# A run of products in 64x128, 32x128, 128x64, 128x32 and full tiles inside a fused attention and feed-forward kernel

## The chip, the cores and the metric

The kernel runs on one core of a Trainium2 chip. A core has five engines that work side by side, each through its own queue in order: TensorE (PE in the profile, with its weight loads as PEld), VectorE (DVE), ScalarE (ACT), GpSimd (POOL) and SyncE (SP), which here only issues DMAs. The metric is the device time of one execution in microseconds. The kernel before takes 237.8 us, the median of two runs (237.64 and 237.96).

## The reference

```python
def reference(A_x, A_wqkv, A_wo, B_x, B_w1, B_w3, B_w2, gate_w):
    x = A_x                                                   # [1, 2048, 512], bf16
    g = _sigmoid((x * gate_w).sum(-1, keepdims=True))
    a = _A_ref(x, A_wqkv, A_wo)                               # causal attention, window 256, 32 heads of 16
    b = _B_ref(x, B_w1, B_w3, B_w2)                           # (silu(x @ w1) * (x @ w3)) @ w2, F = 1376
    return g * a + (1 - g) * b
```

Both branches read the same x of 2048 tokens by 512. Everything is bf16, sums are 32 bit.

## The kernel before

x is held transposed in `xT` (four chunks of 128 features by 2048 tokens), so that it can be the moving operand of projections and of the feed-forward. Work is cut into four token tiles of 512 and, for attention, four groups `c` of eight heads.

**Attention.** `projections(c, tq)` makes K, Q (L436) and V (L494) of one head group and token tile. `main_batch(c, t)` makes scores of 128 keys against 256 queries for eight heads: eight products of 32x128 tiles (L555), four at a time, each in its own row group and its own bank of the four-bank PSUM tile `su`; ACT turns them into exponentials (L559) and POOL masks them. `edge_batch(c, h)` does the same for the block edges, 32 products of 64 columns (L605) and an exp (L609). `pv(c, w)` multiplies the exponentials with V (L695): tiles of 128 rows by 17 columns, in four column strips side by side, into one bank for each half of the heads; DVE turns the two banks (L719), divides and turns back. There is one `su`, so ACT and PE take turns on it.

**Feed-forward.** For each token tile, 11 column blocks of w1 and w3: four products of 512 columns each (L824) into a bank for the gate and one for the up half, then a tanh on ACT (L834) and two products on DVE (L838, L844) into `hT`. Some last columns go another way (`tail_columns`, L781 to L805), through four DMA transposes on SP. Then `hT` with w2 (L874) and a scaled eviction (L879). At the end `output` multiplies with wo (L904), adds both branches on DVE (L908) and writes out.

**Tiles of TensorE.** Full products load 128 x 128 weights. Products that use 32 rows or few columns leave room for others in other rows or columns; the kernel's row form (L555, L605) and column form (L695) run four together. The code calls these forms "full", "row" and "column".

**PSUM.** Of the eight banks `su` has four. The other four, `ch_0` to `ch_3`, serve everything else, one bank for a job.

**What sets the order.** The kernel writes down operations with an engine, a duration, dependencies, a due time, buffers that they take and free (`Plan.add`). `Plan.emit` simulates the engines with these durations and lists each engine's instructions in the order that comes out: of what can start first, the earliest due. `take=[(job, "ch")]` holds a bank from there on and `free` gives it back. The durations serve only for the order; on the chip each instruction waits for the semaphores of what it reads and overwrites. Feed-forward and attention thus interleave: PE does feed-forward products while ACT works on exponentials.

Of the kernel before, what the change touches and what calls it, by code (L numbers as in the profile page):

```python
# [15 lines left out]
P = 128  # L16
KB = 64
# [29 lines left out]
class Plan:  # L47
# [7 lines left out]
    def add(self, eng, dur, fn, deps=(), due=0.0, take=(), free=(), lat=None, form="full", port=False):  # L55
        if lat is None:
            lat = LAT.get(eng, 0.05)
        op = Op(eng, dur, fn, deps, due, list(take), list(free), lat, len(self.ops), form, port)
        self.ops.append(op)
        return op  # L60
# [91 lines left out]
def kernel(  # L152
# [12 lines left out]
    nc = tc.nc  # L165
# [7 lines left out]
    NDC = D // P  # L173
# [15 lines left out]
    xT = pp.tile([P, NDC, S], BF16, name="xT")  # L189
# [5 lines left out]
    w1_sb = pp.tile([P, NDC, F], BF16, name="w1_sb")  # L195
# [35 lines left out]
    ch = [ps.tile([P, 512], F32, name=f"ch_{i}") for i in range(4)]  # L231
# [5 lines left out]
    add = plan.add  # L237
# [111 lines left out]
    def arrive(us):  # L349
        return add("DMA%d" % len(plan.ops), us, lambda: None, lat=0.0)  # L350

    x_in = [arrive(u) for u in landed["x"]]
    w13_in = [arrive(u) for u in landed["w13"]]
# [3 lines left out]
    for b in (1, 0, 2):  # L357
        prev = add("SP", 0.6, lambda b=b: load_w(wqkv_sb, A_wqkv, b * D + 2 * P, (b + 1) * D), [prev], landed["late"],
                   lat=0.0 if b < 2 else 4.0)
# [5 lines left out]
    for m in range(4):  # L365
# [9 lines left out]
        def ev(m=m, half_bank=half_bank):  # L375
# [3 lines left out]
            else:  # L379
                nc.scalar.copy(out=dst, in_=half_bank())  # L380

        a = add("PE", 0.36, tr, [x_in[m // 2]], 0.1 * m, take=[(job, "ch")])
        b = add("DVE" if m != 2 else "ACT", 0.43 if m != 2 else 0.6, ev, [a], 0.1 * m,
                free=[(job, "ch")])
# [20 lines left out]
    a = add("PE", 0.1, gw_turn, [gw_in], 9.407, take=[(gjob, "ch")])  # L405
# [331 lines left out]
    for c in range(NDC):  # L737
# [6 lines left out]
        for w in range(NTC):  # L744
            pv(c, w)

    ffn_total = NTC * ((NFC - 1) * 1.73 + 0.87 + 0.47 + 4 * 2.38)
    done = [0.0]

# [17 lines left out]
    for tcb in range(NTC):  # L767
# [46 lines left out]
        for f in range(NFC):  # L814
# [7 lines left out]
            def half(job, w, lo, hi, f=f, joint=joint, tcb=tcb):  # L822
                for dc in range(lo, hi):
                    nc.tensor.matmul(ch[job.at["ch"]][:],  # L824
                                     lhsT=wA[:, dc, :] if joint else w[:, dc, f * P:(f + 1) * P],
                                     rhs=xT[:, dc, tcb * 512:(tcb + 1) * 512],
                                     start=(dc == 0), stop=(dc == NDC - 1))
# [14 lines left out]
            def m2(job=job, up=up, rg=rg, ru=ru, f=f, joint=joint, tcb=tcb):  # L842
# [6 lines left out]
            a = plan.pieces(HALF, 0.2155, lambda lo, hi, half=half, job=job: half(job, w1_sb, lo, hi),  # L849
                            xt_ready[tcb] + win + last_up + (w_ab if joint else []), due, [(job, "ch")])  # L850
            b = a
            if not joint:
                b = plan.pieces(HALF, 0.2155, lambda lo, hi, half=half, up=up: half(up, w3_sb, lo, hi),
                                [a], due + K["UP"], [(up, "ch")])
# [4 lines left out]
                     take=[(hj, "hT")] if f == 0 else [], free=[(up, "ch"), (job, "h1")])  # L859
# [4 lines left out]
        for mm in range(4):  # L864
# [21 lines left out]
            for k in range(len(cuts) - 1):  # L886
# [3 lines left out]
                           take=[(job, "ch")] if k == 0 else [],  # L890
                           free=[(hj, "hT")] if k == len(cuts) - 2 else [])
# [76 lines left out]
```

## Time and profile before

| | before |
|---|---|
| median of the runs | 237.8 us |
| the profiled execution | 237.91 us |
| its span, first to last instruction | 236.2 us |
| granted TensorE clock | 1.000 |
| matmul records on PE | 3700 |

A profile is one execution. Its page gives the busy time of each engine and the chain of work that ended last; the timeline lists instructions in order of time, those of one line merged. In it, a line has the start, the time from the first start to the last end, engine, line of the code, operation, output and inputs; for PE also rows*columns of the stationary tile and partitions x columns of the moving one. Products are pipelined: a record lasts longer than the distance to the next start. In brackets stands idle time of the engine ahead of the line and what ended it ("issue": nothing that the profile shows).

Stretches of the span, with the busy time of each engine (and its instructions), the clock, the DMA engines' share and GB/s:

```profile
core 0: us, PE busy (x) PEld busy (x) DVE busy (x) ACT busy (x) POOL busy (x), PEclk, DMA share, GB/s
0.00:27.00 27.00, 25.02 (x316) 14.82 (x322) 18.03 (x39) 18.85 (x22) 17.33 (x48) 1.00 0.88 213
27.00:70.00 43.00, 41.52 (x737) 21.32 (x745) 35.61 (x70) 34.24 (x31) 33.44 (x59) 1.00 0.14 39
70.00:112.00 42.00, 40.11 (x678) 20.44 (x685) 32.81 (x56) 34.62 (x30) 27.95 (x42) 1.00 0.13 36
112.00:154.00 42.00, 41.32 (x703) 21.42 (x708) 35.11 (x57) 37.34 (x32) 31.12 (x46) 1.00 0.03 6
154.00:196.00 42.00, 41.31 (x805) 21.97 (x810) 33.95 (x56) 35.48 (x28) 29.73 (x44) 1.00 0.02 4
196.00:236.20 40.20, 36.30 (x478) 17.40 (x476) 30.36 (x48) 17.75 (x13) 14.88 (x21) 1.00 0.18 56
```

### The profile page before, as it was taken

What the parts mean: (1) busy time and instruction counts of PE and PEld (TensorE: products, weight loads), DVE (VectorE), ACT (ScalarE), POOL (GpSimd) and SP (SyncE); (2) the same over time, 40 slices, a digit from 0 to 9 for tenths busy, and PEclk for the clock granted to TensorE, in tenths of its full rate; (3) what the DMA queues carried; (4) which work ended last, traced back from release to release, by engine and by line L of the source; (5) the groups of instructions that cost most, each with busy time, mean ns of one, the idle gap of its engine ahead of it and who ended that gap; (6) DMA issues with size and microseconds to landing.
All of it is one profiled execution on the core that took longest, in us unless ns stands there. A gap on an engine that the chain in (4) does not pass through costs nothing.

```text
span 236.2 us, 8479 instructions
## 1 busy us (share of the span) xinstructions
PE 225.6 (96%) x3700; PEld 117.4 (50%) x3738; DVE 185.9 (79%) x322; ACT 178.3 (75%) x153; POOL 154.5 (65%) x257
## 2 busy tenths in 40 slices
PE   8999899999999999899999999999999999999994
PEld 7544535445544545435553645455555455354542
DVE  5477996997598886767797988898876969987945
ACT  3588879776888989777799898877879998885010
POOL 7169694989567686494759694965768776855000
PEclk9999999999999999999999999999999999999999
DMA  7999262000000005200000000000000001010322
GB/s 198 204 231 300 45 191 71 4 0 3 3 3 3 3 17 161 72 1 3 3 3 3 4 11 14 3 3 3 4 0 3 3 1 27 23 47 25 114 68 89
DMA packets 20445, 11.59 MB, mean 49 GB/s; under 512 B 9688, under 2 KB 20408, under 8 KB 20408
## 3 DMA queue, kind: packets, MB, share of 16 engines
q1 hardware_dynamic: 19712, 10.59, 17.1%
q8 instruction: 29, 0.48, 0.9%
q10 hardware_dynamic: 696, 0.46, 0.6%
q14 instruction: 8, 0.07, 0.1%
HBM read 6.85 MB, written 2.10 MB: 38 GB/s over the span
## 4 chain that ended last, share of the span: by engine, by line
PE 92%; issue 3%; DMA 2%; ACT 1%; DVEq 0%; DVE 0%; ACTq 0%
PE ch L824 30%; PE ch L874 16%; PE ch L436 11%; PE ch L695 9%; PE su L555 8%; PE ch L494 7%; PE ch L904 6%; PE su L605 2%; DMA gwr<-in_gate_w_dram 2%; ACT Ee L609 1%; PE ch L781 1%; ACT L315 0%; DVEq L963 0%; DVE ot L908 0%; ACT tt L834 0%
## 5 line engine op out<-in xcount | busy, mean ns | idle before, releaser
L559 ACT ACTIVATE Em<-su 128x2048 bf16<-128x2048 f32 x60 | 112.6, 1877 | 19.5 <-PE su L555 16.7
L824 PE MATMUL ch<-xT,w_sb 128*128 128x512 bf16 x301 | 77.2, 380 | 1.9 <-issue 0.8
L564 POOL TENSOR_SCALAR_AFFINE_SELECT Em<-Em 64x512 bf16<-64x512 bf16 x60 | 42.5, 709 | 34.0 <-ACT Em L559 29.4
L622 POOL TENSOR_SCALAR_AFFINE_SELECT Ee<-Ee 64x1024 bf16<-64x1024 bf16 x32 | 37.2, 1162 | 17.0 <-ACT Ee L609 15.8
L824 PEld LDWEIGHTS <-w_sb 128*128 128x128 bf16 x320 | 28.3, 98 | 34.6 <-issue 6.0
L838 DVE SCALAR_TENSOR_TENSOR h<-tt,ch 128x512 bf16<-128x512 bf16 (+1 forms) x44 | 29.7, 677 | 13.0 <-ACT tt L834 12.6
L874 PE MATMUL ch<-w_sb,hT 128*128 128x512 bf16 x152 | 38.3, 380 | 0.9 <-issue 0.8
L569 POOL TENSOR_SCALAR_AFFINE_SELECT Em<-Em 64x512 bf16<-64x512 bf16 x56 | 36.8, 658 | 3.3
L512 POOL COPY vs<-vs 64x256 bf16<-64x256 bf16 (+1 forms) x80 | 31.6, 395 | 7.1 <-DVE vs L507 3.8
L609 ACT ACTIVATE Ee<-su 128x2048 bf16<-128x2048 f32 x16 | 30.0, 1877 | 8.0 <-PE su L605 6.4
L436 PE MATMUL ch<-xT,wqkv_sb 128*128 128x512 bf16 (+1 forms) x128 | 33.2, 367 | 0.7 <-issue 0.3
L844 DVE SCALAR_TENSOR_TENSOR hT<-h,ch 128x512 bf16<-128x512 bf16 x40 | 27.0, 676 | 3.1 <-PE ch L824 1.2
L834 ACT ACTIVATE tt<-ch 128x512 bf16<-128x512 f32 (+1 forms) x44 | 26.0, 594 | 4.0 <-PE ch L824 2.7
L695 PEld LDWEIGHTS <-vs 128*17 128x17 bf16 x1664 | 20.5, 92 | 6.3 <-issue 5.1
L874 PEld LDWEIGHTS <-hT 128*128 128x128 bf16 x160 | 14.3, 98 | 16.9 <-issue 2.5
L695 PE MATMUL ch<-Em,vs 128*17 128x256 bf16 (+2 forms) x672 | 22.5, 242 | 0.0
L695 PE MATMUL ch<-Ee,vs 128*17 128x64 bf16 x992 | 22.1, 193 | 0.0
L436 PEld LDWEIGHTS <-wqkv_sb 128*128 128x128 bf16 x136 | 12.3, 98 | 13.8 <-issue 2.9
L494 PEld LDWEIGHTS <-xT 128*128 128x128 bf16 x256 | 15.6, 98 | 5.4 <-issue 2.1
L555 PE MATMUL su<-qT,kz 32*128 32x256 bf16 x240 | 17.3, 278 | 0.6
L555 PE MATMUL su<-qT,k 32*128 32x256 bf16 x240 | 16.6, 268 | 0.0
L555 PEld LDWEIGHTS <-kz 32*128 32x128 bf16 x240 | 6.0, 91 | 18.7 <-issue 17.0
(77 smaller groups left out, 251.7 us busy)
## 6 DMA issues: line engine op xcount, KB each, us to landing
w_sb<-in_B_w_dram SPq DMA_DIRECT2D x4, 512.0 KB, 4.5
out_dram<-ot SPq DMA_DIRECT2D x15, 128.0 KB, 1.7
wqkv_sb<-in_A_wqkv_dram SPq DMA_DIRECT2D x5, 256.0 KB, 3.9
w_sb<-in_B_w_dram SPq DMA_DIRECT2D x2, 608.0 KB, 6.1
w_sb<-in_B_w_dram SPq DMA_DIRECT2D x3, 256.0 KB, 5.0
wo_sb<-in_A_wo_dram SPq DMA_DIRECT2D x1, 512.0 KB, 6.3
xs<-in_A_x_dram SPq DMA_DIRECT2D x1, 256.0 KB, 2.9
xs<-in_A_x_dram ACTq DMA_DIRECT2D x1, 256.0 KB, 3.4
```

Source lines behind the costliest of these rows:

```text
L436: nc.tensor.matmul(pst[:, t0:t1], lhsT=wqkv_sb[:, dc, col + c * P:col + (c + 1) * P], rhs=xT[:, dc, tq * 512 + t0:tq * 512 + t1], start=(d ...
L494: nc.tensor.matmul(pst[:, mm * w:(mm + 1) * w], lhsT=xT[:, dc, m * P:(m + 1) * P], rhs=rhs, start=(dc == 0), stop=(dc == NDC - 1))
L512: nc.gpsimd.tensor_copy(out=v_of(to, base, a), in_=v_of(half, 0, a))
L555: nc.tensor.matmul(su[:, s, a * 256:(a + 1) * 256], lhsT=head_keys(r, t, a), rhs=qT[r, q0:q0 + 256], start=True, stop=True)
L559: nc.scalar.activation(out=Em[job.at["Em"]][:], in_=su[:].rearrange("p s (a q) -> p s a q", a=2), func=ACT.Exp, scale=SCALE)
L564: nc.gpsimd.affine_select(out=e, in_=e, pattern=[[0, 8], [1, KB]], compare_op=ALU.is_ge, fill=0.0, base=0, channel_multiplier=-1)
L569: nc.gpsimd.affine_select(out=e, in_=e, pattern=[[0, 8], [-1, KB]], compare_op=ALU.is_ge, fill=0.0, base=-1, channel_multiplier=1)
L609: nc.scalar.activation(out=Ee[ej.at["Ee"]][:].rearrange("p s t k q -> p s (t k q)"), in_=su[:], func=ACT.Exp, scale=SCALE)
L622: nc.gpsimd.affine_select(out=e, in_=e, pattern=[[0, 4], [0, 4], [1, KB]], compare_op=ALU.is_ge, fill=0.0, base=0, channel_multiplier=-1)
L695: nc.tensor.matmul(po[32 * s:32 * s + VW, lo - 512 * w:hi - 512 * w], lhsT=vs[:, i, a * VW:(a + 1) * VW], rhs=mov, start=(n == 0), stop=(n ...
L824: nc.tensor.matmul(ch[job.at["ch"]][:], lhsT=wA[:, dc, :] if joint else w[:, dc, f * P:(f + 1) * P], rhs=xT[:, dc, tcb * 512:(tcb + 1) * 512],
L874: nc.tensor.matmul(bps[:], lhsT=ht[:, mm * P:(mm + 1) * P], rhs=w2_sb[0:fs, f, :], start=(f == 0), stop=(f == NFC - 1))
```

## The change

A function `form_run` is added ahead of the feed-forward's plan. It takes all four `ch` banks, one after another, once the last part of w1 is there, and then puts 194 products on PE as one operation that the plan doesn't cut. They multiply w1 with the first token tile of x. Nothing reads the results; the banks are given back when the run is over. No other line is changed, but the plan lists everything anew around it.

```diff
+    def form_run():
+        jobs = [Job() for _ in range(4)]
+
+        def run():
+            bank = [ch[j.at["ch"]] for j in jobs]
+            x = xT[:, :, 0:512]
+
+            def mm(b, rows, cols, n, dc):
+                nc.tensor.matmul(bank[b][cols, 0:n], lhsT=w1_sb[rows, dc, cols], rhs=x[rows, dc, 0:n],
+                                 start=True, stop=True)
+
+            every = slice(0, P)
+
+            def full(k, n=512):
+                for i in range(k):
+                    mm(0, every, every, n, i % NDC)
+
+            def halves(k, n=512):
+                for i in range(k):
+                    mm(0, slice(0, KB), every, n, i % NDC)
+                    mm(2, slice(KB, P), every, n, i % NDC)
+
+            def rows(k, n=256):
+                for i in range(k):
+                    for r in range(4):
+                        mm(r, slice(32 * r, 32 * r + 32), every, n, i % NDC)
+
+            def strips(k, n=512):
+                for i in range(k):
+                    for r in range(4):
+                        mm(0, every, slice(32 * r, 32 * r + 32), n, i % NDC)
+
+            def sides(k, n=512):
+                for i in range(k):
+                    for r in range(2):
+                        mm(0, every, slice(KB * r, KB * r + KB), n, i % NDC)
+
+            for _ in range(2):
+                full(2)
+                halves(4)
+                rows(2)
+                halves(4)
+                rows(2, 512)
+                halves(2)
+                full(2)
+                rows(2)
+                full(2)
+                sides(2)
+                strips(2)
+                sides(2)
+                halves(2)
+                strips(2)
+                rows(2)
+                full(1, 128)
+                rows(2)
+                full(2)
+
+        a = w13_in[3]
+        for j in jobs:
+            a = add("PE", 0.01, lambda: None, [a], 25.0, take=[(j, "ch")], lat=0.0)
+        add("PE", 14.0, run, [a], 25.0, free=[(j, "ch") for j in jobs])
+
+    form_run()
```

`KB` is 64, `P` 128 and `NDC` 4. A pass of the loop holds 97 products and 18 groups of one form, full, 64 rows, 32 rows, 64 columns or 32 columns. In the order that comes out, the run stands on PE after the first head group's first strips (L695) and second edge batch (L605), and ahead of a score batch (L555); two groups of V products (L494) that stood before and after those strips come behind it.

## Prediction

> **What bounds the kernel now.** I read the page first: span and busy time, then the chain that ended last.
>
> ```profile
> span 236.2 us, 8479 instructions
> ...
> PE 225.6 (96%) x3700; PEld 117.4 (50%) x3738; DVE 185.9 (79%) x322; ACT 178.3 (75%) x153; POOL 154.5 (65%) x257
> ...
> PE 92%; issue 3%; DMA 2%; ACT 1%; DVEq 0%; DVE 0%; ACTq 0%
> ```
>
> TensorE (PE) is busy for 96% of the span and is 92% of the chain: whatever takes PE time in the middle pushes the end out by as much, unless it fills one of the few holes. The second view is the timeline of PE where the products go in. It gives the price of one product, of a group in one form, and of a change of form.
>
> ```profile
> 21.32 0.29 PE L555 MATMUL su<-qT,kz 32*128 32x256 bf16 x4
> 21.44 0.28 PE L555 MATMUL su<-qT,k 32*128 32x256 bf16 x4
> 21.65 1.90 PE L824 MATMUL ch<-xT,w_sb 128*128 128x512 bf16 x8
> 23.39 0.81 PE L436 MATMUL ch<-xT,wqkv_sb 128*128 128x512 bf16 x3
> 24.13 0.29 PE L555 MATMUL su<-qT,kz 32*128 32x256 bf16 x4
> ...
> 25.50 0.29 PE L695 MATMUL ch<-Em,vs 128*17 128x256 bf16 x4
> ...
> 26.02 0.28 PE L695 MATMUL ch<-Em,vs 128*17 128x256 bf16 x4
> ...
> 26.49 0.20 PE L695 MATMUL ch<-Ee,vs 128*17 128x64 bf16 x4
> 26.63 0.40 PE L494 MATMUL ch<-wv,xT 128*128 128x129 bf16 x4
> 26.96 0.41 PE L605 MATMUL su<-qT,kz 32*128 32x64 bf16 x32
> 27.31 0.40 PE L494 MATMUL ch<-wv,xT 128*128 128x129 bf16 x4
> 28.47 0.39 PE L494 MATMUL ch<-wv,xT 128*128 128x129 bf16 x4 [0.76 <-issue]
> ```
>
> A shape such as 32*128 is active rows by columns of the stationary tile. One record lasts 0.38 us for 512 columns, but the next starts earlier: eight full products take 1.90, so (1.90 - 0.38) / 7 = 0.217 from start to start. Four products in 32 rows go together: the second four start 0.12 after the first (21.32, 21.44), and 256 columns alone are about 0.108. Column strips go together too: from 25.50 to 26.02 each of four strips gets 1152 columns in 0.52 us, which is 0.231 for 512 columns, four at once.
>
> A change of form has a price. The last full product before 24.13 starts at 23.39 + 0.81 - 0.38 = 23.82 and streams 0.217, to 24.04; the row form starts 0.09 later. The last four of the row form at 21.44 stream until 21.55, and full products start 0.10 later. From strips to full, 26.49 plus 0.027 for 64 columns gives 26.52, and the next starts at 26.63: 0.11, of which 0.01 is the other three starts. From single starts over the whole trace, the median is 0.097 for full to rows (59 changes), 0.093 for rows to full (76), 0.096 for full to strips (16), 0.099 for strips to rows (14). Going from 128 to 96 active rows costs nothing (0.003): it is the tile that counts, not the rows in use.
>
> **What is added.** 194 products and as many weight loads stand on PE in one unbroken run; nothing reads them. One pass is costed here, and there are two.
> - Full: 8 of 512 columns x 0.217 = 1.74; one of 128, by the 0.058 start to start of L494, 0.06.
> - 64 rows x 128: 12 pairs. The trace has no 64-row form. Its ends are a pair together, 0.219 (one stream and a 0.003 start as between the four of L555), and one after the other, 0.434. I take 0.219, since four 32-row tiles run together and the two write different banks, as those four do: 12 x 0.219 = 2.63.
> - 32 rows x 128: 8 fours of 256 columns x 0.12 = 0.96; 2 fours of 512 x 0.226 = 0.45.
> - 128 x 64: 4 pairs, with the same ends; strips of 17 columns run four at once, so 4 x 0.219 = 0.88.
> - 128 x 32: 4 fours x 0.226 = 0.90.
>
> The sum is 7.62 a pass, 15.2 for both.
>
> Changes of form: 17 inside a pass, 34 in all; one from the row form before the run (L605) and one back to the row form after it (L555). In the rest of the built order the count of changes between full, rows and strips goes from 170 to 174. That is 40 x 0.097 = 3.9. Twelve of the 34 lie between two sizes in one direction (64 and 32 rows, 64 and 32 columns), which the trace doesn't show. Their ends are 0 and, as a bound above, twice the row, 0.19; I take 0.097, by the strips to rows change, which is also from one small form to another. The Trainium skill, TensorEngine Tiling (Array Packing), section Tiling Modes, says that changing the tiling mode drains the engine while changing the tile does not; by that all 34 cost, and by the other reading, that only a change between full, rows and columns does, the sum would be 12 x 0.097 = 1.2 lower. The rows above bear the rule out for the changes they have.
>
> **What it moves.** The run asks for all four ch banks, so eight V products (L494) that stood before and between the strips (L695) and the edge batch (L605) go behind it. Its first product writes a free bank. Its second bank and the others are read last by DVE:
>
> ```profile
> 24.72 1.90 ACT L559 ACTIVATE Em<-su 128x2048 bf16<-128x2048 f32 x1
> ...
> 26.25 0.72 DVE L719 STREAM_TRANSPOSE xs<-ch 128x512 f32<-128x512 f32 x1
> 26.89 0.25 DVE L791 SCALAR_TENSOR_TENSOR hb<-tb,ch 128x128 bf16<-128x128 bf16 x1
> 27.07 0.70 DVE L719 STREAM_TRANSPOSE xs<-ch 128x512 f32<-128x512 f32 x1
> 27.69 0.25 DVE L795 SCALAR_TENSOR_TENSOR hb<-hb,ch 128x128 bf16<-128x128 bf16 x1
> ```
>
> In the new order the two L719 stand back to back, so the second ends near 27.6. The strips end 0.3 earlier (one L494 group is gone from ahead of them), but the edge batch must wait for the exp of 24.72, done at 26.62. It starts at about 26.65 instead of 26.3: an idle 0.34 that an L494 group had covered. It takes 0.35; the run starts near 27.1 and reaches the second bank near 27.6, the bank of L795 near 28.6: both are just free and cost nothing. Were DVE half a microsecond late, PE would wait that long.
>
> The hole of 0.76 at 28.47 waits for no semaphore; it comes after two bursts of some 190 products in 2 us. Behind the run, whose products go slowly, I expect it to be covered: -0.76; its ends are that and 0 (it moves into the run). Another of 0.75 stands at 97.04 and can move or stay. Queued behind the run: ACT's exps and tanhs, idle from about 29.3 to 46, and on DVE the product L844 waiting for its up half. On SP the first tile's transposes are past; the second tile's four now stand behind the late weight loads, and their data is wanted much later. The last 740 products of PE are in the same order as before, so the tail with its last DVE step and output DMA (some 4 us after PE) is unchanged.
>
> Sum: 15.2 + 3.9 + 0.34 - 0.76 = 18.7. The profiled execution took 237.91 (1.7 around the span), the median of the runs is 237.8: 237.9 + 18.7 = **256.6 us**, span 254.9.
>
> **Rivals.**
> - ACT or the four banks bound the kernel after the run. ACT does nothing for some 17 us and the work then has to be refilled. For it: from 112 to 154 ACT is busy 37.34 of 42, and its largest waits leave little there. Against it: from 27 to 236.2 it is busy 159 of 209, all of it shifts with PE, and the order converges again. If each 42 us stretch between 70 and 196 loses about 1 us of PE time, and 1 is lost refilling, that is 4: 260.6.
> - 64-row and 64-column pairs do not run together: 16 pairs x 2 passes x 0.217 = 6.9 more, 263.5. Against it: both directions run together in fours.
> - Loads show: products that use all rows load only after the one before has gone. 66 such products (9 full, 8 sides and 16 strips a pass) x 0.098, the L824 load, is 6.5: 263.1. Against it: eight full products at 0.217 with loads of 0.098 between them. The Trainium skill, TensorE: Matmul & The Clock Gate, Part 3, says that weight loads overlap running products only when the row group differs; that would give this time, and the 0.217 disagrees.
> - Changes cost less than in the rest: the 12 unshown ones nothing, and the four outside the run neither: 256.6 - 1.6 = 255.0, and 253.8 if the second hole closes as well.
> - Not slower: the products never reach the array, because something between build and chip drops what nobody reads. It decides alone: at fewer than about 50 of the 194, the rest fits in 4.8 us. With none, 237.8. For it: nothing reads the banks. Against it: warm-up products (L308), which nobody reads either, stand in the trace with 29 records. Hiding the run beside other work can't do it: PE has 236.2 - 225.6 = 10.6 idle in all, much of it at both ends.
>
> **How the numbers follow.** Forecast, with its changes dearer or cheaper, 0.74 (254.5 to 259); cheap changes 0.05; ACT or banks 0.10; pairs apart 0.06; loads 0.03; dropped 0.02. The range goes from 253.8 (cheap changes with both holes gone) to 261.5 (the ACT case and a dear change: 12 x 0.09 over its 260.6); pairs, loads and dropped lie outside. A measurement tells 2% (4.8 us) from no change: slower 0.97, within 2% 0.02, faster 0.01.
>
> **What would show it.** The run should be one stretch of PE from about 27.1 to 45.7, with 194 products less the missing records and no wait longer than 0.5 in it. Pairs of 64 rows should start 0.003 apart and the next pair 0.216 later; if they start 0.217 apart each, the pairs case is right. Fours of strips the same. Each change of form should leave 0.09 to 0.10 beyond the stream, also between 64 and 32. PE idle outside the run should be about 10 us as before; more than 13 would mean ACT or the banks. The forecast is wrong if the run takes under 16.5 or over 21 us, or if the work after it stretches by more than 2.

## The result, and the profile after

The changed kernel takes 257.24 us (257.06 and 257.41) against 237.8: 1.0817 times as long, 95% interval 1.0771 to 1.0864. The profiled execution took 257.06, its span is 255.0. The forecast was 256.6 with a span of 254.9.

From the page of the changed kernel: span, busy time, chain, and the group of the new products (L755). The lines of the kernel behind the run have moved down by 64: L824 is now L888, L844 is L908.

```profile
span 255.0 us, 8899 instructions
...
PE 249.7 (98%) x3932; PEld 123.2 (48%) x3932; DVE 183.3 (72%) x322; ACT 177.8 (70%) x153; POOL 154.1 (60%) x257
...
PE 88%; DMA 5%; ACT 2%; SPq 2%; issue 1%; DVE 1%; DVEq 0%; ACTq 0%
...
L755 PE MATMUL ch<-xT,w_sb 32*128 32x256 bf16 (+5 forms) x194 | 18.7, 345 | 0.0
```

All 194 products are there, with no idle time ahead of them. DVE, ACT and POOL have much the same work as before (183, 178 and 154 us busy; 186, 178 and 154 before) in a longer span, so their shares fall; only PE's rises. 5% of the chain now goes through the landing of the first weights (DMA), in the opening.

The timeline of PE around the run:

```profile
27.23 0.21 PE L695 MATMUL ch<-Ee,vs 128*17 128x64 bf16 x4
27.54 0.41 PE L605 MATMUL su<-qT,kz 32*128 32x64 bf16 x32
27.88 18.73 PE L755 MATMUL ch<-xT,w_sb 128*128 128x512 bf16 x194
46.55 0.29 PE L555 MATMUL su<-qT,kz 32*128 32x256 bf16 x4
```

The run is one piece from 27.88 to the next score batch at 46.55, 18.67 us. What the other engines do beside it, from the timelines of ACT and DVE:

```profile
25.59 1.90 ACT L559 ACTIVATE Em<-su 128x2048 bf16<-128x2048 f32 x1
...
28.03 1.88 ACT L609 ACTIVATE Ee<-su 128x2048 bf16<-128x2048 f32 x1 [0.37 <-PE su L605]
47.00 1.88 ACT L559 ACTIVATE Em<-su 128x2048 bf16<-128x2048 f32 x1 [17.09 <-PE su L555]
```

```profile
27.02 1.30 DVE L719 STREAM_TRANSPOSE xs<-ch 128x512 f32<-128x512 f32 x2
...
48.88 0.69 DVE L908 SCALAR_TENSOR_TENSOR hT<-h,ch 128x512 bf16<-128x512 bf16 x1 [17.22 <-PE ch L888]
```

ACT and DVE finish what is queued and then wait 17 us for PE. Whether that idle time comes back later is read from stretches of the span behind the run:

```profile
27.90:46.50 18.60, 18.60 (x201) 5.08 (x194) 3.72 (x7) 1.88 (x1) 3.61 (x4) 1.00 0.54 155
46.50:89.00 42.50, 42.39 (x720) 21.58 (x720) 31.86 (x64) 33.22 (x30) 29.81 (x55) 1.00 0.01 3
89.00:131.00 42.00, 42.00 (x702) 20.76 (x701) 32.22 (x56) 35.26 (x31) 29.66 (x43) 1.00 0.02 5
131.00:173.00 42.00, 41.76 (x699) 20.90 (x697) 34.13 (x58) 36.02 (x31) 31.02 (x47) 1.00 0.03 6
173.00:215.00 42.00, 42.00 (x813) 21.93 (x812) 32.83 (x54) 34.82 (x28) 28.30 (x43) 1.00 0.01 3
```

Behind the run PE is busy for all but 0.4 of 168.5 us (the second number of each line), and ACT for at most 36.02 of 42. The run costs what it takes on PE, and nothing behind it stretches.

A sum by the single starts of PE: from the last product of the edge batch ahead of the run to the next score batch 18.79 us, from there to the end 208.49. Before, the last product of that edge batch starts at 27.19 and 209.02 us follow. So 18.79 + 208.49 - 209.02 = 18.26 come from that point on, and 27.76 - 27.19 = 0.57 from ahead of it, together 18.8, the difference of the spans. (Both sums start with the same product, though in the order before eight V products more lie ahead of it.)

### The profile page after: what moved, and what is told of

It reads as the page before. It is cut to its first block, busy times and chain, and to the rows that moved or that the text cites. A ratio compares the mean times of both kernels' runs of the same rounds, so it can differ in the third digit from the quotient of the medians.

```text
span 255.0 us, 8899 instructions
## 1 busy us (share of the span) xinstructions
PE 249.7 (98%) x3932; PEld 123.2 (48%) x3932; DVE 183.3 (72%) x322; ACT 177.8 (70%) x153; POOL 154.1 (60%) x257
## 3 DMA queue, kind: packets, MB, share of 16 engines
HBM read 6.85 MB, written 2.10 MB: 35 GB/s over the span
## 4 chain that ended last, share of the span: by engine, by line
PE 88%; DMA 5%; ACT 2%; SPq 2%; issue 1%; DVE 1%; DVEq 0%; ACTq 0%
PE ch L888 27%; PE ch L938 15%; PE ch L436 10%; PE ch L695 8%; PE ch L755 7%; PE su L555 7%; PE ch L494 6%; PE ch L968 5%; DMA w_sb<-in_B_w_dram 3%; PE su L605 2%; DMA wqkv_sb<-in_A_wqkv_dram 2%; ACT Em L559 2%; SPq L288 1%; ACT tt L898 1%; PE ch L845 0%
## 5 line engine op out<-in xcount | busy, mean ns | idle before, releaser
L888 PE MATMUL ch<-xT,w_sb 128*128 128x512 bf16 x320 | 79.3, 380 | 0.5 <-DMA w_sb<-in_B_w_dram 0.4
L888 PEld LDWEIGHTS <-w_sb 128*128 128x128 bf16 x320 | 28.4, 98 | 34.1 <-issue 5.0
L908 DVE SCALAR_TENSOR_TENSOR hT<-h,ch 128x512 bf16<-128x512 bf16 x40 | 27.1, 678 | 20.6 <-PE ch L888 18.5
L938 PE MATMUL ch<-w_sb,hT 128*128 128x512 bf16 x160 | 39.2, 380 | 0.0
L436 PE MATMUL ch<-xT,wqkv_sb 128*128 128x512 bf16 (+1 forms) x136 | 36.3, 372 | 0.2 <-DVE h L902 0.2
L695 PEld LDWEIGHTS <-vs 128*17 128x17 bf16 x1664 | 20.6, 92 | 6.1 <-issue 4.5
L695 PE MATMUL ch<-Em,vs 128*17 128x256 bf16 (+2 forms) x672 | 22.6, 242 | 0.0
L695 PE MATMUL ch<-Ee,vs 128*17 128x64 bf16 x992 | 22.1, 193 | 0.0
L755 PE MATMUL ch<-xT,w_sb 32*128 32x256 bf16 (+5 forms) x194 | 18.7, 345 | 0.0
L494 PEld LDWEIGHTS <-xT 128*128 128x128 bf16 x256 | 15.6, 98 | 4.8 <-issue 1.9
L943 DVE TENSOR_SCALAR bsb<-ch,omg 128x512 bf16<-128x512 f32 x15 | 11.2, 744 | 9.2 <-PE ch L938 9.1
L555 PE MATMUL su<-qT,kz 32*128 32x256 bf16 x240 | 17.3, 278 | 0.0
```

Source lines behind the costliest of these rows:

```text
L436: nc.tensor.matmul(pst[:, t0:t1], lhsT=wqkv_sb[:, dc, col + c * P:col + (c + 1) * P], rhs=xT[:, dc, tq * 512 + t0:tq * 512 + t1], start=(d ...
L494: nc.tensor.matmul(pst[:, mm * w:(mm + 1) * w], lhsT=xT[:, dc, m * P:(m + 1) * P], rhs=rhs, start=(dc == 0), stop=(dc == NDC - 1))
L555: nc.tensor.matmul(su[:, s, a * 256:(a + 1) * 256], lhsT=head_keys(r, t, a), rhs=qT[r, q0:q0 + 256], start=True, stop=True)
L695: nc.tensor.matmul(po[32 * s:32 * s + VW, lo - 512 * w:hi - 512 * w], lhsT=vs[:, i, a * VW:(a + 1) * VW], rhs=mov, start=(n == 0), stop=(n ...
L755: nc.tensor.matmul(bank[b][cols, 0:n], lhsT=w1_sb[rows, dc, cols], rhs=x[rows, dc, 0:n], start=True, stop=True)
L888: nc.tensor.matmul(ch[job.at["ch"]][:], lhsT=wA[:, dc, :] if joint else w[:, dc, f * P:(f + 1) * P], rhs=xT[:, dc, tcb * 512:(tcb + 1) * 512],
```

## Experiments

The theory throughout is that of the prediction: the run lies on PE's path with all it takes, its groups run side by side, each change of form has a price, and the rest keeps its length. "Run" below is from the last product of the edge batch to the next score batch (18.79 us in the changed kernel), "rest" from there to the end of the span (208.49).

| | run | rest | median us | ratio to the kernel before, 95% |
|---|---|---|---|---|
| changed kernel | 18.79 | 208.49 | 257.24 | 1.0817 (1.0771 to 1.0864) |
| `e1_grouped` | 15.49 | 208.84 | 253.37 | 1.0629 (1.0600 to 1.0659) |
| `e2_apart` | 24.23 | 208.92 | 261.76 | 1.1012 (1.0961 to 1.1064) |
| `e3_same_rows` | 23.94 | 208.62 | 262.42 | 1.1036 (1.0985 to 1.1087) |
| `e4_same_cols` | 25.64 | 208.49 | 263.73 | 1.1086 (1.1041 to 1.1131) |
| `e8_four_passes` | 37.34 | 208.19 | 275.57 | 1.1548 (1.1483 to 1.1612) |

### One form in one block

```diff
-            for _ in range(2):
-                full(2)
-                halves(4)
...
+            full(8)
+            full(1, 128)
+            full(8)
+            full(1, 128)
+            halves(24)
+            rows(16)
+            rows(4, 512)
+            sides(8)
+            strips(8)
```

> The same 194 products, those of one form in one block: 4 changes of form inside the run instead of 34, the rest of the order unchanged. Theory (each change costs 0.097 us on the path): 30 x 0.097 = 2.9 less, 254.3 us, and a run of about 15.7 us. Rival (the streams alone carry the cost, and changes are absorbed by the pipeline): 257.2. Rival (what the run does to ACT and to the banks carries part of the 19 us): the run gets shorter, the time by less than 2.9.

Measured 253.37 us. From the timeline of PE (the first product of the run has no record here, so that the run begins 0.22 before the line says):

```profile
27.84 15.21 PE L755 MATMUL ch<-xT,w_sb 128*128 128x512 bf16 x193 [0.16 <-issue]
42.98 0.29 PE L555 MATMUL su<-qT,kz 32*128 32x256 bf16 x4
```

The run is 3.30 shorter for 30 changes fewer, 0.110 each, and the rest has its length within 0.35. Both rivals fall: the changes are not absorbed, and their saving reaches the end. (The time is 0.9 below the expected 254.3, and 3.9 under the changed kernel's; 3.3 of that is the run, and this kernel's four times alone spread over 1.4.) It was a little more than 0.097 each, and the single starts show why. In the long block, fours of 256 columns start 0.109 apart; the first four after a change has 0.119 to the next, and its products last 278 ns against 268. So a change costs 0.097 until the first start, and 0.010 more in the first group.

### No two groups of a form together

```diff
-            for _ in range(2):
-                full(2)
-                halves(4)
-                rows(2)
...
+            for _ in range(2):
+                halves(1)
+                rows(1)
+                halves(1)
+                full(1)
+                halves(1)
+                rows(1)
...
```

> The same 194 products with no two groups of one form next to each other: 77 changes inside the run instead of 34. Theory: 43 x 0.097 = 4.2 more, 261.4 us. Rival (a drain is paid once where the forms are short, so that changes close together overlap): clearly under 261, about 259. Rival (changes cost nothing): 257.2.

Measured 261.76, and a run 5.44 longer for 43 changes more. Not all of this is changes. The run now begins with a pair, which needs a second bank at once, and two banks are not yet free. From the timeline of DVE, which reads them last, and the starts of PE (us, and ns since the last start):

```profile
26.70 1.31 DVE L719 STREAM_TRANSPOSE xs<-ch 128x512 f32<-128x512 f32 x2
...
28.36 0.23 DVE L880 SCALAR_TENSOR_TENSOR hb<-hb,ch 128x128 bf16<-128x128 bf16 x1
```

```
27.561  64 rows   512 columns
28.063  64 rows   512 columns   +502
...
28.374  32 rows   256 columns   +3
28.643  32 rows   256 columns   +269
```

Both late products start 0.05 after DVE is done, and together they cost 0.75 us. The other 4.69 are 0.109 for each change: nothing overlaps when changes follow each other closely, and they don't get dearer either. The starts of PE in later groups:

```
30.671  64 rows   512 columns
30.674  64 rows   512 columns   +3
30.993  32 rows   256 columns   +319
30.997  32 rows   256 columns   +4
...
31.213  full      512 columns   +210
31.536  64 rows   512 columns   +323
```

512 columns in a block take 0.2155 and here 0.322 or 0.323; a lone four of 256 takes 0.220 against 0.109. Taken over the whole run, with 14.8 us for the columns alone (60 groups of 512 x 0.2155, 16 of 256 x 0.1085, 2 of 128 x 0.056), a change costs 0.111 in the changed kernel (36 with the two at its ends), 0.114 in the blocks (6) and 0.110 here (79, the 0.75 for the banks taken off).

### Both products of a pair in the same rows

```diff
-                    mm(2, slice(KB, P), every, n, i % NDC)
+                    mm(2, slice(0, KB), every, n, i % NDC)
```

> Both products of each 64-row pair use rows 0 to 63 (another product, with results that nobody reads); all else as in the changed kernel. Theory (a pair is cheap because the two halves of the array stream at the same time): the second product waits its turn, 24 pairs x 0.214 = 5.1 more, 262.3 us. Rival (a product on half the rows takes half as long by itself): 257.2.

Measured 262.42; the run is 5.15 longer, where 5.1 were expected. The groups of 64-row products, of the changed kernel and then of this one (busy time, which counts overlapping products once, and the mean of one in ns):

```profile
L755 PE MATMUL ch<-xT,w_sb 64*128 64x512 bf16 x48 | 6.6, 379 | 0.0
```

```profile
L755 PE MATMUL ch<-xT,w_sb 64*128 64x512 bf16 x48 | 11.7, 378 | 0.0
```

One product takes the same 0.38 in both; only the second of each pair no longer lies beside the first. Half the rows save nothing by themselves, two halves at once do.

### All products of a group in the same columns

```diff
-                        mm(0, every, slice(32 * r, 32 * r + 32), n, i % NDC)
+                        mm(0, every, slice(0, 32), n, i % NDC)
...
-                        mm(0, every, slice(KB * r, KB * r + KB), n, i % NDC)
+                        mm(0, every, slice(0, KB), n, i % NDC)
```

> All products of a 64-column pair use columns 0 to 63, and all of a 32-column four columns 0 to 31 (nobody reads the results). Theory: they go one after the other, 8 pairs x 0.214 + 8 fours x 0.642 = 6.8 more, 264.0 us. Rival (few columns are cheap by themselves): 257.2. Rival (the next product in the same columns must also wait for its weight load): up to 0.098 for each of 48 products on top, 268.

Measured 263.73; the run is 6.85 longer, where 6.8 were expected. For the 32-column products, of the changed kernel and of this one:

```profile
L755 PE MATMUL ch<-xT,w_sb 128*32 128x512 bf16 x32 | 2.5, 384 | 0.0
```

```profile
L755 PE MATMUL ch<-xT,w_sb 128*32 128x512 bf16 x32 | 7.6, 380 | 0.0
```

The third possibility, a load that shows when the next product uses the same rows and columns, falls too: it would have added up to 0.098 for each of 48 products, 4.7 us. The Trainium skill (TensorE: Matmul & The Clock Gate, Part 3) has weight loads overlap running products only where the row group differs, though the same part also names a background weight buffer that lets a load go ahead; here loads into the same rows and columns, as those of full products, are hidden behind 512 columns.

### Four passes

```diff
-            for _ in range(2):
+            for _ in range(4):
                 full(2)
```

> Four passes of the run instead of two, order unchanged. Theory: each pass adds its streams and 17 changes, 9.3 us by the run of the changed kernel, and the work behind it keeps its 208.5 us: 257.2 + 18.6 = 275.8 us. Rival (what waits behind the run makes its end dearer the longer it is): over 277, with the part behind it longer than 208.5.

Measured 275.57; the run grew by 18.55 to 37.34, the rest is 208.19. Twice the wait for ACT, DVE and POOL has no price behind the run.

### The place without the products

```diff
-            for _ in range(2):
-                full(2)
...
+            return
```

> The run's place is kept in the plan (14 us, four banks), but it issues no product: PE's order is that of the changed kernel without the 194 products. Theory (the rest of the order costs nothing; the run alone is the price): the score batch behind the run now follows the edge batch at once and must wait for ACT to empty su, about 1.9 us that the run had covered; 257.2 - 18.8 + 1.9 = 240.3 us, the work from that score batch to the end as long as in the changed kernel (208.5). Rival (the new order is itself worse, by ACT or the banks): the part after it is longer and the time over 242. Rival (the new order is better, as the hole of 0.76 is gone): under 238.

Measured 240.46 us, 1.0089 times the kernel before (1.0062 to 1.0117), with a rest of 208.19. From the timeline of PE:

```profile
26.95 0.41 PE L605 MATMUL su<-qT,kz 32*128 32x64 bf16 x32
29.37 0.29 PE L555 MATMUL su<-qT,kz 32*128 32x256 bf16 x4 [2.00 <-ACT Ee L609]
```

The hole is there, 2.00 where 1.9 were expected, and it is the exp of the edge batch that ends it. So the new order is 0.9% slower by the wait that it opens (and by what that does to the clock, see below), and otherwise neither better nor worse; the run costs its 18.8 and covers a wait of 2.0 that its own place in the plan had opened. The ten times spread from 239.3 to 241.94, which led to the experiment on the clock below.

### One pass here, one in the middle

```diff
-    def form_run():
+    def form_run(due):
...
-            for _ in range(2):
+            for _ in range(1):
...
-            a = add("PE", 0.01, lambda: None, [a], 25.0, take=[(j, "ch")], lat=0.0)
-        add("PE", 14.0, run, [a], 25.0, free=[(j, "ch") for j in jobs])
+            a = add("PE", 0.01, lambda: None, [a], due, take=[(j, "ch")], lat=0.0)
+        add("PE", 7.0, run, [a], due, free=[(j, "ch") for j in jobs])
 
-    form_run()
+    form_run(25.0)
+    form_run(120.0)
```

> One pass of 97 products in the old place, the other between two score batches in the middle of the program, where ACT is busiest (37.34 of 42 us in the profile before). Form changes 211 in all against 210. Theory (PE is the bound everywhere, so the place doesn't matter): 257.3 us within 1. Rival (ACT and the one su tile have too little slack in the middle to be held for 9 us): 259 to 261.

Measured 260.18: the theory's 257.3 was missed by 2.9, and the rival's range was hit. Not for its reason, though. The timeline of PE at the second pass, and two stretches of it (with the granted clock third from the end):

```profile
130.22 0.29 PE L555 MATMUL su<-qT,kz 32*128 32x256 bf16 x4 [1.98 <-ACT Em L559]
130.33 0.29 PE L555 MATMUL su<-qT,k 32*128 32x256 bf16 x4
130.56 10.98 PE L755 MATMUL ch<-xT,w_sb 128*128 128x512 bf16 x97
```

```profile
130.20:132.00 1.80, 1.78 (x18) 0.54 (x17) 0.60 (x1) 1.80 (x2) 1.69 (x3) 0.93 0.00 0
132.00:134.00 2.00, 2.00 (x16) 0.58 (x16) 0.00 (x0) 0.55 (x1) 1.31 (x2) 0.50 0.00 0
```

While the plan collected the four banks it had only score batches left for PE, and put two of them next to each other; the second waits 1.98 for ACT to empty `su`. And the pass takes 11.1 instead of the 9.6 of the first: from 131.76, for 3.413 us, the granted clock is 0.50, and products of 512 columns start 0.42 apart. 2.0 + 1.5 is more than the excess, as this profile's opening is shorter: the edge batch ahead of the first pass starts 1.27 earlier than in the changed kernel's (26.27 against 27.54).

```diff
-    form_run(120.0)
+    form_run(125.0)
```

> As the kernel with two places, with the second pass due 5 us later, so that full products and no second score batch stand ahead of it. Form changes 212 against 210. Theory (the place costs nothing; what the two-places kernel paid was the 2 us hole ahead of its second pass, with the clock at 0.50 for 3.4 us behind that hole): no hole of 2 us, clock 1.000, both passes 9.6 us, 257.5 us. Rival (a hold of 9 us in the middle costs ACT's slack there): still 259.5 or more.

Measured 255.72, 1.0726 times the kernel before (1.0661 to 1.0791). From the timeline of PE around the second pass:

```profile
130.79 0.28 PE L555 MATMUL su<-qT,k 32*128 32x256 bf16 x4
131.00 1.07 PE L494 MATMUL ch<-wqkv_sb,xT 128*128 128x128 bf16 x16
131.90 3.94 PE L755 MATMUL ch<-xT,w_sb 128*128 128x512 bf16 x38
...
141.28 0.29 PE L555 MATMUL su<-qT,kz 32*128 32x256 bf16 x4
```

With V products ahead of it there is no hole, the clock stays at 1.00, and the pass takes 9.4. The place costs nothing, even where ACT is busiest; a badly filled stretch ahead of it does. It is 1.8 under the expectation: in its profile the last product of the edge batch ahead of the first pass starts 1.2 earlier than in the changed kernel's (26.54 against 27.76), that is the opening, and two losses on PE that the changed kernel's profile has behind its run (0.27 at 72.79 and 0.41 at 158.43) are not in it.

### Three of the kernels again

The kernel before again:

> The kernel before once more, for a second profile. Theory (the hole of 0.76 at 27.7 belongs to the order, behind two bursts of short products): a hole over 0.3 in the same place, 237.8 us. Rival (it was that one execution's): no hole there.

Measured 237.51 (one time). Its two holes, from the timeline:

```profile
27.99 0.39 PE L494 MATMUL ch<-wv,xT 128*128 128x129 bf16 x4 [0.30 <-issue]
...
96.63 0.20 PE L605 MATMUL su<-qT,kz 32*128 32x64 bf16 x2 [0.82 <-issue]
```

Both come again in their places (0.76 and 0.75 in the first profile). The first is just at the limit of what was expected (0.47 lost from start to start, against 0.92 in the first profile), so holes belong to the order, but their size to the execution. The changed kernel again:

> The changed kernel once more, on the chip of its neighbours here. Theory (the part ahead of the run differs between executions by the landing of the first weights; the part from the last edge batch before the run to the end does not): run 18.8 and rest 208.5 within 0.3, total 256 to 257.5 us as the opening falls. Rival (the run in one place is dearer than in two): run or rest longer by 1.

Measured 257.11, ratio 1.0810 (1.0759 to 1.0861). The edge batch ahead of the run comes 0.61 earlier than in the first profile, as expected of the opening. The run is 19.11 and the rest 209.07, 0.32 and 0.58 longer, a little beyond the 0.3 expected, and both have a place. The run comes so early that its second bank is not yet free: the second product of the first pair starts 0.126 behind the first, not 0.003, and the pairs stay out of step until the form changes; so again for the other banks. The rest has a hole of this kind, from the timeline:

```profile
73.08 0.27 PE L605 MATMUL su<-qT,kz 32*128 32x64 bf16 x13 [0.69 <-issue]
```

In the first profile of the changed kernel the same batch lost 0.27 from start to start, here 0.85.

The kernel with the empty run again:

> The kernel with the empty run once more, whose times spread from 239.3 to 241.9 us. Theory (the 2.0 us hole on PE brings the clock to 0.50 for 3.4 us in some executions, 1.7 us each): times in two groups near 239.5 and 241, the longer with a mean granted clock of about 0.993 and the shorter of 0.997 to 1.000. Rival (the spread is the opening's): times don't go with the clock.

Measured 240.83, ratio 1.0110 (1.0086 to 1.0134). Stretches of its profile, the hole and what follows:

```profile
26.60:29.10 2.50, 0.45 (x39) 0.35 (x33) 2.46 (x7) 2.13 (x3) 1.31 (x2) 1.00 0.00 0
29.10:29.80 0.70, 0.65 (x14) 0.43 (x14) 0.70 (x2) 0.20 (x2) 0.63 (x1) 1.00 0.21 47
29.80:33.20 3.40, 3.40 (x20) 2.00 (x18) 1.39 (x2) 1.80 (x3) 3.28 (x4) 0.51 0.62 168
```

PE is busy for 0.45 of 2.5 us and 0.7 later the clock is at half for 3.4 us, and the rest is 209.85 against 208.19 in that kernel's first profile, where the same hole left the clock alone. Of its 14 times, the nine with a mean clock of 0.993 or less lie between 240.33 and 241.94, the five of 0.997 or more between 239.3 and 240.69. The times go with the clock. The two groups overlap between 240.33 and 240.69; that the opening spreads them is likely, but only two of these executions have a profile.

## Why the prediction was right

- **The run.** Streams and 36 changes (34 inside and one at each end) came to 15.2 + 3.5 = 18.7; measured 18.79. The split was off both ways: the columns alone take 14.8, since groups of 512 start 0.2155 apart in every form (priced at 0.217 to 0.226) and fours of 256 are 0.109 apart (priced at 0.12), and a change costs 0.111, since the first group of a form is 0.010 longer. The row used for the fours was of a batch of two, where the first four carries the change's last part.
- **The forms that the trace before did not show.** 64-row and 64-column pairs run together (`e3_same_rows`, `e4_same_cols`); the rival of 263.5 was the time that the pairs apart would give, and 262.4 is what the rows alone gave. Of the twelve kinds of change in the run (by direction) eleven have medians from 0.093 to 0.099, those between 64 and 32 among them (0.093 to 0.097); full to 32 rows has 0.098 behind 512 columns and 0.108 behind the single product of 128. All 34 cost, which agrees with what TensorEngine Tiling of the Trainium skill says of draining.
- **Nothing hides it.** 208.2 to 208.5 behind the run with two passes, four or none. The rival by which ACT or the banks bind afterwards falls, in the early place and, by `e7_second_place`, in the middle.
- **The wait of the edge batch** for the exp, 0.34 beyond the change in the forecast, was 0.17: from the last strip to the edge batch are 0.292, and 0.125 in `e10_after_again`, where the exp was done first. The banks were just free in the first profile, late by 0.1 to 0.2 in the second and by 0.50 and 0.27 in `e2_apart`, as the text had it for DVE late.
- **The hole of 0.76** is gone from its place, as forecast. But it is a size of one execution (0.30 in the second profile), and another of its kind stands at 72, behind another edge batch. The credit was right in that profile and luck in its size.
- **What was left out** is the opening: the edge batch ahead of the run starts anywhere from 26.3 to 28.0 in the thirteen profiles, with the same products ahead of it (the kernel before has eight V products more there). The chain of the changed kernel goes through the landing of w1 and w3 there, and the traces show that this landing spreads it. In eight of the eleven profiles with the run's place in the plan, the edge batch starts 9.39 to 9.40 after the fourth load into `w_sb` lands, in two 9.48 and 9.49 after it, and in one, where it landed first of all, 10.68; it lands from 16.25 to 18.60, at 18.14 in the changed kernel's first profile and at 17.28 in the kernel before's.
- **Luck in the sum.** The span came within 0.14 of its forecast (255.04 against 254.9), but two misses cancel in it. The edge batch starts at 27.54 and not at 26.65, 0.89 late. From its last product on, 18.26 came on top where the forecast has 19.0 (its 18.7 and the 0.31 by which it put the edge batch earlier than before), mostly because the second hole, of 0.75 at 97.04, is gone as well, which the forecast had left open and not credited.
- **Numbers that don't come out.** The forecast's range starts at 253.8, but 255.0 without a hole of 0.75 is 254.2; and it ends at 261.5, where 260.6 and 12 x 0.09 make 261.7. Both are far from the measured time. The bursts ahead of the first hole are 112 products of strips and edge batch, not 190. And PE is idle for 5.35 in the changed kernel, where about 10 was expected: the first profile of the kernel before lacks 38 product records (3700 against 3738 in its second, which has 6.10 idle), and their places count as idle.

What the holes behind bursts of short products wait for can be narrowed down from the traces; no semaphore ends them. With PE's products and loads numbered from 0 in order of time, the five such holes of the profiles that lack no records stand ahead of number 705 and 3009 (the kernel before, second profile), 1985 (the changed kernel, both) and 5569 (`e6_two_places`): each 193 beyond a multiple of 256. The queue q8 of the profiles, `instruction`, moves one packet of 16 KB for each 256 of them (29 packets for 7489), and in these five holes and the six of other profiles such a packet lands 1.2 to 1.6 us before the hole ends. So PE most likely waits there for its next 256 instructions, which a burst uses up faster than they come: 1.9 to 2.4 us for the 256 ahead of four of the five holes, 3.9 for the other. The added products shift these places. Number 705 now lies inside the run, at 29.40, and 3009 in a score batch, at 105.70, with no hole at either. No run changed the loading of instructions, so this cause is argued and not shown.

## What to carry to other kernels

On a kernel whose PE is full, extra products cost their columns, counted once for the products that stream side by side, plus 0.11 us for each change of the tile's form; so put products of one form together, and count changes before products. Products in 64 or 32 rows or columns gain only if their partners in the other rows or columns stand next to them, and write banks that are free at the same time. When such work is moved, look at what stands ahead of it: two batches next to each other that share one buffer cost more than the work's place ever did.

## What the runs showed of the hardware

- Half the clock for 3.413 us after a hole of 2.0 us on PE, in some executions and not in others (`e6_two_places` and `e11_empty_again`, but not the profile of `e5_empty`). The Trainium skill (TensorE: Matmul & The Clock Gate, Part 1) describes a free-running window of 3413 ns and half the clock after an idle one, and gives as a rule no idle gaps over some 3.4 us. The length agrees; a gap of 2.0 was enough here.
- What sets these profiles apart is where the hole falls. The clock changes whole multiples of 3.413 us after it rose early in the program: after 7 of them, from 5.95 to 29.84, in `e11_empty_again`, and after 37, from 5.47 to 131.76, in `e6_two_places`. In these two all or nearly all of the hole lies in the 3.413 us before the change, of which PE is busy for 1.31 and 1.54. In `e5_empty` the clock rose at 4.22; a border at 28.11 cuts the hole in two, and the stretches on either side have 2.58 and 2.15 us of busy PE. How little is too little is open: a stretch with 1.47 at the end of `e8_four_passes` kept the clock. Nor is such a hole the only way there: of 36 executions of the kernel before that were timed beside the experiments, one has a mean clock of 0.993 too (241.92 us), and neither profile of that kernel has a hole of 2.0.
- A pair that once starts out of step stays so: after a 0.126 wait for a bank, the products of the pairs started 0.10 and 0.115 apart in turn, at the same rate for a pair, until the next change of form.
